# A new table of order, slots and engines for a fused attention and feed-forward kernel

## The chip, the core and the metric

The kernel runs on one core of one Trainium2 chip. The metric is device microseconds of one execution. The core has a matrix engine (TensorE, PE in the profile, with its weight loads as PEld), VectorE (DVE), ScalarE (ACT), GpSimd (POOL) and SyncE (SP, which here only issues DMAs). POOL and ACT issue DMAs too.

## The reference

Random-feature attention over 8 batches and 8 heads of 576 tokens and 64 channels, followed by a feed-forward layer without a gate:

```python
def phi(x):
    proj = np.einsum('bhsd,df->bhsf', x, w_phi)
    proj = proj - np.max(np.abs(proj), axis=-1, keepdims=True)
    return np.concatenate([np.exp(proj), np.exp(-proj)], axis=-1)
q_p, k_p = phi(q), phi(k)
kv = np.einsum('bhsf,bhsd->bhfd', k_p, v)
z = np.sum(k_p, axis=2)
num = np.einsum('bhsf,bhfd->bhsd', q_p, kv)
den = np.einsum('bhsf,bhf->bhs', q_p, z)[..., None] + 1e-06
attn = num / den
...
h = np.maximum(np.maximum(x @ w1, x @ w2), x @ w3)
return h @ w_out
```

`x` is `attn` with 4608 rows (8 batches of 576 tokens) of 512; `w1`, `w2`, `w3` are 512 by 768, `w_out` is 768 by 512.

## The kernel before, in words

**Units and chunks.** The attention is cut into 16 units (two per batch, four heads each) and the feed-forward part into 9 chunks (one per batch of 512 tokens, and a last one of the 64 tokens that are left in each batch). The body of the kernel does not issue instructions: it makes a graph of 1479 steps (`Node`), each with a function that issues its instructions, the engines that may do it, and the buffers that it uses.

**A unit.** q, k and v are loaded (L452 through POOL's queue with a cast to bf16 for units 1 to 3, L463 through SP's queue in f32 for the others and for every v; L441 for the first unit). For units 0 to 3 TensorE turns q and k (L483) and DVE copies them out (L486); for later units POOL casts them (L469) and a DMA turns them (L498). TensorE then projects (L525 and L520, step G), ACT makes exp of k's projections (`Ek`, L538), DVE takes the row maxima of both (L544). From k's maxima ACT makes the factor `em` (L575); v is multiplied by it (`va`, L579, two of 128 by 1152 elements a unit, four of half the width in units 0 and 1), and the factor itself is copied into the 65th column (`vd`, L589). TensorE sums k's features with that product (step K, L633, 72 small matmuls); the result is copied out (`kv`, L638). q's maxima are turned and written into a row of `qkT` by a small DMA (step V, L560), q is projected a second time (L604; L606 and L609 in units 0 and 1) and exponentiated by ACT (`Eq`, L617); TensorE multiplies with `kv` (step N, L651), DVE divides (L657, L658), and the result is turned (L671, or a DMA at L681).

**A chunk.** The maximum of three products is written as w1's product plus the larger of 0, w2's minus w1's, and w3's minus w1's. So `w2 - w1` and `w3 - w1` are formed once (`wd`, L775: three column pieces each, both operands in SBUF), w1 is turned (step wt, L787, copied out by `we`, L790) and multiplied with `w_out` (step wm, L801). A chunk is then 12 steps of four 128x512 matmuls (L704), whose results are cut at 0 (`t1`, L714 on DVE or L712 on ACT) or joined (`h`, L710), and four times a straight product (L732) and a product with `w_out` (L737), copied out (`osb`, L745) and stored (L752).

**The weights** come by four DMAs of 768 KB through POOL's queue with a cast (`w_load`, L413): nodes 1081 (w1), 1082 (w2), 1083 (w3) and 1084 (w_out).

**The order.** A constant string, `PLAN`, holds one word per step. `1087G@37.9` says: node 1087, on POOL (G; T is TensorE, D DVE, A ACT, S SP), at place 37.9; digits and letters between engine and place are the slots of the buffers that it is the first to use. `plan` (L243) reads the words, `fill` (L261) sorts the steps by their places, adds idle 128x512 matmuls (L832) in places where TensorE's row has a hole, and calls the steps' functions in that order. So the numbers after `@` are not waited for: they set each engine's order of instructions, and every engine works through its own order, waiting for what an instruction needs. A DMA's place sets its place in its queue, and SP, POOL and ACT issue in order, too.

**Gates.** v's load of units 1 to 3 is held back by a one-element DVE copy (`gate`, L461, nodes 86, 159 and 231) that writes into v's buffer after an earlier unit's `qkT` is there. SP waits for it before it issues that load and everything behind it.

Of the kernel before, what the change touches and what calls it, by code (L numbers as in the profile page):

```python
# [48 lines left out]
VA_DVE = 1  # L49
# [46 lines left out]
0G@0.5 1G@1.2 4A@2.0 2D0@0.8 10S0@0.7 3D@1.1 11D0@4.2 6S0@1.3 7D@5.0 15T1@5.6 5D@5.5 16D0@6.4 86D0@7.2 26T002300@7.2 12S@1.9  # L96
13A@5.8 8S@2.6 9A@6.5 27A@7.6 28A@8.2 29D@7.6 19T4@7.5 20D@8.2 17T5@7.6 18D@8.4 21T67@8.3 24D@9.0 23A@8.7 41T1@8.6 43A@9.2
22A@9.6 36T24@9.2 37A@10.0 39D@9.6 31T56@9.8 44D@10.3 34D@10.6 32A@10.5 38A@11.0 33A@11.5 25D@11.2 45D@11.8 84G1@1.7
40D@12.1 57T20@11.3 58A@12.0 42A@12.5 85G@2.5 90T5@11.8 91D1@12.8 59A@12.8 14S1@3.2 54T7@12.4 55A@13.3 63T4@12.9 64A@13.8
56A@14.3 35D@13.4 50A0@14.8 65A@15.0 104T111211@13.5 66T5@13.8 158G2@3.4 68A@15.5 108D@14.0 30D@14.6 46A@15.8 88T6@14.1  # L100
89D@15.2 92T7@14.9 93D@15.8 107D@16.0 60T3@15.3 61A@16.1 94T46@16.0 98D@16.6 105A@16.6 67A@17.1 99T71@16.8 102D@17.2
96A@17.4 62A@17.9 97D@17.9 101A@18.4 157G@4.2 163T5@17.6 164D2@18.5 1081G@5.1 1091T7@18.1 1092D0@19.1 109T34@18.7 112D@20.2
161T0@19.0 1084G@5.9 106A@18.9 110A@19.4 95A@19.9 1095T5@19.6 1096A@20.3 114T2@20.0 117D@20.8 116A@21.3 103D@21.2 162D@21.8
111A@21.7 1093T7@20.4 52G0@15.2 47G@16.3 115A@22.1 53G@17.4 49G@17.7 51G@18.0 48G@19.1 69T063@21.0 71A@22.5 133T51@22.1
134A@22.9 70A@23.4 130T0@22.6 159D2@22.4 113D@22.5 118D@23.1 1094D@23.5 100A@23.8 135A@24.3 230G0@20.2 1082G@21.0 229G@21.8
74T30@23.0 75D0@24.6 1083G@22.7 119A1@24.8 122G1@25.1 132A@25.0 78T4@23.4 127T2@23.7 136T6@24.1 137A@25.5 72T1@24.6
73D1@25.2 79D0@25.8 182T007500@25.0 185D@26.5 184A@26.0 138A@26.5 123A@26.9 186D@27.1 1099T3@25.4 1100D@27.7 1101T1@26.7
1102D@28.3 131A@27.2 129A@27.7 177T46@28.1 87S@7.4 120G@25.4 121G@26.5 172T70@28.3 175D@28.9 76T3@28.6 183A@28.2 128A@28.7
165T5@28.9 166D@29.5 178A@29.1 173A@29.6 179A@30.1 139T1@29.1 174A@30.6 1103T2@29.3 140A@31.1 1104A@31.4 180D@29.7 77D1@30.3
181D@31.0 187T7@30.6 191D@31.6 126G@27.7 125G@27.9 124G@29.1 142T154@30.9 176D@31.9 144A@32.1 141A@32.5 143A@32.9 367S1@17.2  # L110
370G1@30.2 167T36@31.9 171D@32.5 195A0@33.3 169A@33.5 189A@34.0 198A0@34.4 188A@34.5 1085G@31.3 235T2@32.3 236D0@33.1
170D@33.7 82T0@32.9 80T4@33.1 81A@34.9 145T11@33.4 146D0@34.3 147T5@33.8 148D1@35.0 190D@35.6 1097T2@34.1 168A@35.5 83A@36.0
1098A@36.6 149T3@35.4 150D0@35.9 151T1@35.7 152D1@36.5 233T4@36.0 234D@37.2 254T115711@36.6 256A@37.1 237T6@37.0 238D@37.8
257D@38.0 153T3@37.1 192T0@37.4 193A0@37.7 231D3@38.6 154A@37.9 155T2@37.5 156A@38.6 255A@39.2 160S@22.6 197G@33.7
244T14@37.9 247D@38.7 196G@35.8 214T006@38.2 216A@39.7 215D@39.4 245A@40.1 249T35@39.2 250A@40.6 252D@39.8 239T21@39.5
242D@40.4 240A@41.1 251A@41.6 258D@41.0 1090D@41.6 241A@42.1 1107T0@39.9 366S1@27.2 259T6@40.8 263D@42.2 1087G@37.9
1115T3@41.0 1116A1@42.5 1108A@43.0 261A@43.5 246A@43.9 1109T2@41.9 253D@42.5 369G@40.0 1088D@43.1 1117T7@42.7 1118A@44.4
302S0@32.6 305G2@41.1 194S@38.1 199T30@43.6 211T5@43.8 212A@44.9 213A@45.4 200A@45.7 243D@43.8 262D@44.4 248D@44.7
1129T0@43.9 1130D@45.3 1086G@42.2 1111T1@44.8 208T7@45.6 1112D@45.9 1110D@46.5 209A@46.2 267A1@46.7 264T4@45.9 265A1@46.9
# [12 lines left out]
412A@65.9 1141A2@66.4 409A@67.0 311D@66.0 330D@66.6 295T5@65.7 411A@67.5 408A@68.0 331D@67.1 296D1@67.4 291T6@66.0
292D0@68.0 1143T4@66.3 289T7@67.2 290D1@68.6 436S0@62.3 303S2@65.2 496S1@65.8 329A@68.5 498S3@66.5 1144T@67.5 1145D3@69.3
308A@68.8 416T1@68.8 418A@69.3 413T5@68.9 415A@69.7 299T2@69.1 300A@70.2 297T6@69.4 298D@69.9 417A@70.8 317T07@69.8
320D@70.4 321D@71.0 695G2@64.4 403G@65.5 401G@65.8 419T034@70.0 421D@71.6 499G0@71.6 332T6@71.2 333D1@72.0 334S@72.3
335A1@71.7 338G1@72.7 337G@73.0 420D@72.2 1155T2@71.2 1167T0@72.1 1156D0@72.6 1168D@73.3 319A@72.0 414A@72.5 318A@73.0
447T001400@73.1 449A@73.5 452T63@73.3 455D@73.9 453A@74.0 437T52@73.5 439A@74.5 448A@75.0 438A@75.5 454A@75.9 440D@74.5
450D@75.1 441D@76.1 1157T7@73.9 1158A@76.4 1165T0@74.7 457T6@75.6 459A@76.9 428T50@75.8 429D0@76.7 566S1@73.0 628S1@75.9
451D@77.3 461D@77.9 1153T1@76.1 1154A@77.3 1166D@78.3 1149T2@77.0 442T75@77.9 443A@78.4 445D@78.9 1150A@78.9 458A@79.4
444A@79.7 336G@75.1 354T114@78.2 356A@80.2 355D@79.5 424T0@79.3 348T21@79.6 349A@80.6 460D@79.9 425D1@80.2 350A@81.2  # L140
627S1@76.5 630G1@82.3 497S0@77.2 500G@83.8 345T7@79.8 456D@80.8 446D@81.4 1169T1@80.1 1170D@82.0 342T6@80.9 587T11411@81.1
343A@81.7 589A@82.2 426T0@81.4 590D@82.7 339T3@81.7 341A@82.5 433S2@77.8 465A0@83.0 467G0@85.3 466G@87.4 340A@83.3 344A@83.8
1146S@79.1 691S0@80.3 694G@89.5 1147T2@81.9 1148D@83.0 422T5@82.7 423D0@83.6 427D1@84.3 430S@85.0 347A@84.2 1159T1@83.1
# [142 lines left out]
def kernel(  # L286
# [133 lines left out]
    def attention(u):  # L420
# [84 lines left out]
        em = buf("em", 2, [P, 2, UT], FP32)  # L505
# [62 lines left out]
        for t0, t1, need in ranges:  # L568
            def va(*args):
                n_va.append(nd(*args))  # L570
                return n_va[-1]
# [10 lines left out]
            for g in range(2):  # L582
                costs = {"POOL": 0.14 + 0.1085 * (t1 - t0)}
                if VA_DVE > u:
                    costs["DVE"] = 0.11 + 0.105 * (t1 - t0)
# [172 lines left out]
    w_nodes = []  # L758
# [105 lines left out]
```

## Time and profile before

| | |
|---|---|
| time, three runs | 291.24, 291.28, 291.81 us; median 291.28 |
| span of the profiled execution, first to last instruction | 290.5 us |
| what lies around the span, against the median | 0.78 us |
| TensorE busy | 276.3 us of the span |
| DVE, ACT, POOL busy | 213.8, 193.8, 116.9 us |

The profile is one execution. Busy time of an engine leaves out the time in which it waits. A window is a stretch of the span; its row gives the busy time of each engine in it with the number of instructions, the granted TensorE clock (1.00 is full speed), the mean busy share of the DMA engines and GB/s. The waits list says who waited for whom: time in total, times, longest. In a timeline row stand start, length, engine, line, operation and tiles; in brackets the idle time ahead of it and what ended it.

### The profile page before, as it was taken

How to read it: one execution, taken by the hardware profiler on the slowest of the kernel's cores; microseconds unless marked ns; L12 is line 12 of the kernel's file. 1: busy time of each engine (PE TensorE's matmuls, PEld its weight loads, DVE VectorE, ACT ScalarE, POOL GpSimd, SP SyncE). 2: the span in 40 equal slices, each digit the busy share in tenths (PEclk: the TensorE clock that was granted, in tenths of full speed). 3: DMA queues.
4: the chain of work that ended last, by engine and by line, in shares of the span. 5: the costliest groups of instructions: out<-in, count | busy, mean ns of one | idle time of the engine just before them, and what ended most of it. 6: DMA issues, size and time to landing. Idle time of an engine off the chain costs nothing.

```text
span 290.5 us, 8509 instructions
## 1 busy us (share of the span) xinstructions
PE 276.3 (95%) x3518; PEld 157.4 (54%) x3555; DVE 213.8 (74%) x449; ACT 193.8 (67%) x446; POOL 116.9 (40%) x99
## 2 busy tenths in 40 slices
PE   8678999899999999999999999999999999999995
PEld 3447676356656655555555566555544654444443
DVE  5695899998998967988979879878963382455411
ACT  1795989789898989976797898858758510021021
POOL 8055789728373662817180753500077001000000
PEclk9997999999999999999999999999999999999999
DMA  7999967899999999997999545982240109414045
GB/s 184 280 242 199 246 198 181 197 360 212 231 241 361 150 257 253 275 262 157 225 324 273 118 83 156 164 167 45 52 115 2 39 10 208 91 39 95 12 122 170
DMA packets 65649, 50.83 MB, mean 175 GB/s; under 512 B 46154, under 2 KB 50378, under 8 KB 65610
## 3 DMA queue, kind: packets, MB, share of 16 engines
q1 hardware_dynamic: 61279, 45.03, 63.2%
q0 software_dynamic: 4000, 4.92, 9.9%
q8 instruction: 28, 0.46, 0.6%
q10 hardware_dynamic: 331, 0.33, 0.3%
q14 instruction: 11, 0.09, 0.1%
HBM read 34.67 MB, written 9.44 MB: 152 GB/s over the span
## 4 chain that ended last, share of the span: by engine, by line
PE 66%; DMA 13%; DVE 10%; POOL 5%; issue 2%; SPq 2%; ACT 2%; ACTq 0%; POOLq 0%; DVEq 0%
PE ups L704 22%; PE ops L737 13%; PE ops L732 9%; DMA w_bf<-in_moe_w_dram 6%; PE psn L651 5%; DMA qkT<-qk_bf 5%; PE kvps L633 5%; PE psm L604 3%; PE psq L525 3%; DVE mk L544 3%; DVE hT L710 2%; POOL vab L579 2%; DMA q_raw<-in_q_dram 2%; DVE mqp L544 2%; PE pm L801 2%
## 5 line engine op out<-in xcount | busy, mean ns | idle before, releaser
L704 PE MATMUL ups<-xT,w_bf 128*128 128x512 bf16 x412 | 101.7, 379 | 2.5 <-DVE mk L544 0.9
L617 ACT ACTIVATE Eq<-psm 128x512 bf16<-128x512 f32 (+1 forms) x160 | 82.3, 584 | 9.6 <-PE psm L604 8.2
L579 POOL TENSOR_TENSOR vab<-v_raw,em 128x1152 bf16<-128x1152 f32 (+1 forms) x36 | 67.9, 1904 | 44.6 <-ACT em L575 31.7
L538 ACT ACTIVATE Ek<-psk 128x512 bf16<-128x512 f32 x128 | 70.6, 616 | 8.3 <-PE psk L525 5.1
L704 PEld LDWEIGHTS <-w_bf 128*128 128x128 bf16 x432 | 40.6, 98 | 47.2 <-issue 2.3
L544 DVE TENSOR_REDUCE mqp<-psq 128x4 bf16<-128x512 f32 (+1 forms) x80 | 48.8, 632 | 8.3 <-PE psk L525 4.9
L737 PE MATMUL ops<-wout_bf,hT 128*128 128x512 bf16 (+1 forms) x215 | 50.4, 373 | 0.4
L710 DVE TENSOR_TENSOR hT<-hT,ups 128x512 bf16<-128x512 bf16 x54 | 35.9, 681 | 12.3 <-PE ups L704 8.5
L544 DVE TENSOR_REDUCE mk<-psk 128x4 f32<-128x512 f32 x64 | 42.6, 682 | 1.8 <-PE psk L525 1.1
L745 ACT COPY osb<-ops 128x512 f32<-128x512 f32 (+1 forms) x18 | 10.5, 590 | 38.2 <-PE ops L737 35.7
L737 PEld LDWEIGHTS <-hT 128*128 128x128 bf16 x222 | 21.0, 98 | 22.3
L658 DVE TENSOR_TENSOR x_sb<-psn,rden 128x320 bf16<-128x320 f32 x64 | 31.5, 491 | 2.2
L712 ACT ACTIVATE hT<-ups 128x512 bf16<-128x512 f32 x32 | 19.8, 627 | 17.2 <-PE ups L704 17.2
L651 PEld LDWEIGHTS <-Eq 128*128 128x128 bf16 x640 | 25.2, 97 | 7.7
L651 PE MATMUL psn<-kv_sb,Eq 128*128 128x65 bf16 x640 | 27.3, 194 | 0.0
L745 DVE COPY osb<-ops 128x512 f32<-128x512 f32 (+1 forms) x19 | 12.8, 673 | 19.5 <-PE ops L737 16.4
L732 PE MATMUL ops<-xT 128*128 128x512 bf16 x89 | 24.0, 380 | 0.4
L525 PE MATMUL psq<-w,qkT 64*128 64x128 bf16 x256 | 21.5, 219 | 0.8 <-DMA qkT<-qk_bf 0.8
L604 PE MATMUL psm<-qkT,wphi_m 128*128 128x512 bf16 (+1 forms) x70 | 22.3, 358 | 0.0
L525 PE MATMUL psk<-w,qkT 64*128 64x128 bf16 x256 | 21.4, 219 | 0.0
L714 DVE TENSOR_SCALAR hT<-ups 128x512 bf16<-128x512 f32 x22 | 14.8, 685 | 8.4 <-PE ups L704 8.4
L633 PE MATMUL kvps<-vab,Ek 64*128 64x65 bf16 x1152 | 20.1, 190 | 0.4 <-POOL vab L579 0.4
(76 smaller groups left out, 266.7 us busy)
## 6 DMA issues: line engine op xcount, KB each, us to landing
v_raw<-in_v_dram SPq DMA_DIRECT2D x16, 576.0 KB, 5.4
out_dram<-osb SPq DMA_DIRECT2D x66, 128.0 KB, 2.4
k_raw<-in_k_dram SPq DMA_DIRECT2D x12, 576.0 KB, 4.5
q_raw<-in_q_dram SPq DMA_DIRECT2D x12, 576.0 KB, 6.0
w_bf<-in_moe_w_dram POOLq DMA_DIRECT2D x3, 768.0 KB, 17.0
qk_bf<-in_q_dram POOLq DMA_DIRECT2D x3, 288.0 KB, 10.9
qk_bf<-in_k_dram POOLq DMA_DIRECT2D x3, 288.0 KB, 10.7
wout_bf<-in_moe_w_out_dram POOLq DMA_DIRECT2D x1, 768.0 KB, 21.0
```

The costliest lines, as they stand in the source:

```text
L525: nc.tensor.matmul(ps()[:, i, :], lhsT=cols[r, :], rhs=w2[r, c, :], start=True, stop=True)
L538: nc.scalar.activation(Ek[s]()[:, tiles_of(t0, n), :], of(1), EXP, scale=1.0 - 2.0 * s)
L544: nc.vector.tensor_reduce((mq, mk)[c]()[:, tiles_of(t0, n)], of(c), AXX, ALU.max, apply_absolute_value=True)
L579: (nc.vector if n_.eng == "DVE" else nc.gpsimd).tensor_tensor(vab()[:, g, t0:t1, 0:D], vb()[:, t0:t1, :], em()[:, g, t0:t1].unsqueeze(2).t ...
L617: nc.scalar.activation(Eqb()[s][:, cols], psm()[:, 0:w], EXP, scale=1.0 - 2.0 * s)
L633: nc.tensor.matmul(kvps[ab]()[:, t // NT, g, :], lhsT=Ek[g]()[r, t, :], rhs=vab()[r, g, t, :], start=(t + g == 0), stop=(t == UT - 1 and g ...
L651: nc.tensor.matmul(psn()[:, c, :], lhsT=Eqb()[g][:, t0:t0 + P], rhs=kv()[:, pr, ab, g, :], start=(g == 0), stop=(g == 1))
L658: nc.vector.tensor_tensor(x_sb()[:, pr, :, ab, :], psn()[:, :, 0:D], rden().to_broadcast([P, 5, D]), ALU.mult)
L704: nc.tensor.matmul(ups(), lhsT=w_bf[i + 1][:, ct, j * P:(j + 1) * P], rhs=tokens_of(ct), start=(ct == 0), stop=(ct == CT - 1))
L710: nc.vector.tensor_tensor(hT()[:, j, :], hT()[:, j, :], ups(), ALU.max)
L732: nc.tensor.matmul(ops_()[:, 0:width], lhsT=tile_of(ct, tt), rhs=line_w[c_i > MOVE][:, ct, cols], start=(ct == 0), stop=False)
L737: nc.tensor.matmul(ops_()[:, 0:width], lhsT=hT()[:, j, tt * P:(tt + 1) * P], rhs=wout_bf[:, j, cols], start=False, stop=(j == JT - 1))
```

## The change

All words of `PLAN` are replaced; two kinds of steps get more engines to choose from. Nothing else in the code differs, and the arithmetic is the same. The table is cut here to the words that the texts speak of:

```diff
-VA_DVE = 1
...
 PLAN = """
-... 84G1@1.7 ... 85G@2.5 ... 158G2@3.4 ... 157G@4.2 ... 1081G@5.1 ... 1084G@5.9 ... 230G0@20.2 ... 1082G@21.0 ... 229G@21.8 ... 1083G@22.7 ...
-... 86D0@7.2 ... 87S@7.4 ... 367S1@17.2 ... 159D2@22.4 ... 160S@22.6 ...
+... 84G0@1.9 ... 85G@2.6 ... 1081G@3.3 ... 157G1@4.0 ... 158G@4.7 ... 1084G@5.5 ... 1082G@6.2 ... 229G2@11.4 ... 230G@12.1 ... 1083G@12.8 ...
+... 86D1@20.2 ... 87S@20.4 ... 159D2@20.9 ... 367S1@20.9 ... 160S@21.3 ... 432S0@21.8 ... 366S1@22.2 ...
...
             for g in range(2):
-                costs = {"POOL": 0.14 + 0.1085 * (t1 - t0)}
-                if VA_DVE > u:
-                    costs["DVE"] = 0.11 + 0.105 * (t1 - t0)
+                costs = {"POOL": 0.14 + 0.1085 * (t1 - t0), "DVE": 0.11 + 0.064 * (t1 - t0)}
                 n_ = va("va", costs, None, [n_em, mains[2]], [vb, em, vab])
...
-            n_ = va("vd", {"ACT": 0.15, "POOL": 0.28}, None, [n_em], [em, vab])
+            n_ = va("vd", {"ACT": 0.15, "POOL": 0.28, "DVE": 0.15}, None, [n_em], [em, vab])
...
-            n_ = node("wd", 0, {"DVE": 0.6} if i else {"POOL": 2.1}, None, [w_nodes[0], w_nodes[i + 1]], [])
+            n_ = node("wd", 0, {"DVE": 1.2, "POOL": 2.1}, None, [w_nodes[0], w_nodes[i + 1]], [])
```

What the two tables say, counted:

| step | before | after |
|---|---|---|
| `va`, product of v (L579) | POOL 36 | POOL 29, DVE 7 (one each in units 8, 9, 10, 11, 14, two in unit 15) |
| `vd`, copied column (L589) | POOL 9, ACT 9 | POOL 9, ACT 6, DVE 3 |
| `wd`, weight differences (L775) | POOL 3, DVE 3 | POOL 5, DVE 1 |
| `kv` (L638) | DVE 17, ACT 15 | DVE 7, ACT 25 |
| `t1` (L714, L712) | DVE 22, ACT 32 | DVE 18, ACT 36 |
| `osb` (L745) | DVE 19, ACT 18 | DVE 16, ACT 21 |
| casts of unit 0 (L445) | DVE 2, ACT 2 | ACT 4 |
| step V's DMA (L560) | SP 13, ACT 1 | SP 10, ACT 4 |
| last chunk's stores (L752), and idle matmuls (L832) | 1 on ACT; 23 | 3 on ACT; 31 |

Order in the queues at the start, read from the two built programs:

| queue | before | after |
|---|---|---|
| POOL's DMAs | two loads of unit 1, two of unit 2, w1, w_out; then, behind unit 0's four `va`: unit 3's k, w2, unit 3's q, w3 | two loads of unit 1, w1, two of unit 2, w_out, w2, two of unit 3, w3; then unit 0's `va` |
| SP, behind unit 0's loads | v of unit 1 (gate 86, seventh of DVE's steps), k of unit 5, v of unit 2 (gate 159), q of unit 5, k of unit 4 | v of unit 1 (gate 86, 26th of DVE's steps, behind most of unit 1's maxima), k of unit 5, v of unit 2, k of unit 6, q of unit 5 |

288 lines of the change are left out of this document (147 added, 141 removed).

## Prediction

> **What bounds the kernel now.** I read the page first, then the windows, to see in which part of the span TensorE is not full. The page has a span of 290.5 us, against a median time of 291.28 us; the 0.78 us between them is taken as what lies around the span, and put back at the end.
>
> ```profile
> span 290.5 us, 8509 instructions
> PE 276.3 (95%) x3518; PEld 157.4 (54%) x3555; DVE 213.8 (74%) x449; ACT 193.8 (67%) x446; POOL 116.9 (40%) x99
> PEclk9997999999999999999999999999999999999999
> ```
>
> ```profile
> core 0: us, PE busy (x) PEld busy (x) DVE busy (x) ACT busy (x) POOL busy (x), PEclk, DMA share, GB/s
> 8.00:20.40 12.40, 9.81 (x167) 6.21 (x167) 10.10 (x20) 11.16 (x28) 2.68 (x5) 1.00 1.14 266
> 20.40:27.00 6.60, 4.16 (x55) 3.34 (x50) 2.80 (x5) 3.11 (x7) 5.03 (x6) 0.74 1.20 199
> 27.00:70.00 43.00, 41.44 (x739) 26.30 (x743) 40.46 (x85) 38.73 (x95) 29.77 (x22) 1.00 0.91 230
> 70.00:150.00 80.00, 78.36 (x1149) 46.39 (x1157) 69.66 (x154) 69.11 (x162) 43.04 (x33) 1.00 1.00 251
> 150.00:245.00 95.00, 93.83 (x1183) 52.72 (x1196) 69.65 (x146) 63.57 (x147) 30.54 (x23) 1.00 0.53 110
> ```
>
> From 27 us on TensorE is idle for 1.56 of 43, 1.64 of 80 and 1.17 of 95 us: it is the bound, and its work is the same in both tables, so no order can win more than some 4 us there. The weak place is the window from 20.4 to 27: 4.16 busy of 6.60, at a mean clock of 0.74, with DVE and ACT mostly idle as well. The timeline and the waits of that stretch say why.
>
> ```profile
> 22.98 0.77 PEld L787 LDWEIGHTS <-w_bf 128*128 128x128 bf16 x8 [2.60 <-DMA w_bf<-in_moe_w_dram]
> ...
> 27.01 1.27 PE L633 MATMUL kvps<-vab,Ek 64*128 64x65 bf16 x72
> ```
>
> ```profile
> 4.96 17.97 DMA w_bf<-in_moe_w_dram
> ```
>
> ```profile
> ACT Ek L538 <- PE psk L525: 2.7, 1, 2.7
> DVE hT L790 <- PE pwT L787: 2.5, 1, 2.5
> DVE mqp L544 <- PE psq L520: 1.3, 1, 1.3
> ACT hT L790 <- PE pwT L787: 0.7, 1, 0.7
> ```
>
> TensorE stands for 2.60 us in front of the first turning of w1 (L787); w1 was issued at 4.96 and landed 17.97 us later, at 22.93. ACT and DVE run dry behind it. Unit 0's K (L633), the mark by which I compare the two tables, starts at 27.01.
>
> **The change, part by part.**
>
> *A, the start.* The new table issues w1 third on POOL's queue instead of fifth, and holds v of unit 1, and so all loads behind it on SP, until the 26th of DVE's steps, instead of the seventh. What the queues moved, in the DMA view cut to 0 to 10.5, 10.5 to 18.5, 18.5 to 23 and 30 to 42 us (packets, MB, share; q0 is POOL's queue, q1 SP's):
>
> ```profile
> q1 hardware_dynamic: 793, 1.67, 52.6%
> q0 software_dynamic: 439, 0.49, 29.4%
> ...
> q0 software_dynamic: 796, 0.92, 66.2%
> q1 hardware_dynamic: 597, 1.28, 46.7%
> ...
> q0 software_dynamic: 748, 0.93, 118.3%
> ...
> q0 software_dynamic: 903, 1.22, 56.9%
> q1 hardware_dynamic: 816, 1.77, 41.8%
> ```
>
> A load of a unit's q or k is 0.295 MB in q0, a weight 0.786. Before, w1 ends at 4 x 0.295 + 0.786 = 1.97 MB: 0.49 + 0.92 are done at 18.5, the rest at 0.93 / 4.5 = 0.207 MB/us takes until 21.2, and the landing is seen 1.7 us later. After, w1 ends at 2 x 0.295 + 0.786 = 1.38 MB. The 1.28 MB of q1 from 10.5 to 18.5 are mostly the two loads that are now held, so q0 has the DMA engines to itself: 10.5 + 0.89 / 0.207 = 14.8, landing at about 16.5. With q1 as busy as before it would be 10.5 + 0.89 / 0.115 + 1.7 = 19.9. The turning stands three steps earlier in TensorE's order, which was done with all in front of it at 20.38, so it comes to it little before 17, and the 2.60 us go.
>
> The lost clock goes with it: (1 - 0.74) x 6.60 = 1.7 us. Together 4.3. What is late next are ACT and DVE: the table asks for as many DVE steps ahead of unit 0's K as before (31), and ACT was 11.16 of 12.40 busy ahead of the stall. They can only win what they waited: ACT 2.7 + 0.7, DVE 2.5 + 1.3. I take **-3.7**, near the 3.8 of DVE; bounds -4.3 and -1.3 (w1 at 19.9, a stall and a slow clock remain). [...]
>
> *B, differences off DVE.* Two of three `wd` leave DVE.
>
> ```profile
> 47.96 0.96 DVE L775 TENSOR_TENSOR w_bf<-w_bf 128x1024 bf16<-128x1024 bf16 x1
> 49.77 1.68 DVE L775 TENSOR_TENSOR w_bf<-w_bf 128x1024 bf16<-128x1024 bf16 x1
> 55.29 1.63 DVE L775 TENSOR_TENSOR w_bf<-w_bf 128x1024 bf16<-128x1024 bf16 x1
> ...
> 47.23 1.15 POOL L469 CAST qk_bf<-k_raw 128x1152 bf16<-128x1152 f32 x1
> 48.34 2.57 POOL L775 TENSOR_TENSOR w_bf<-w_bf 128x1024 bf16<-128x1024 bf16 x1
> 50.85 1.60 POOL L469 CAST qk_bf<-k_raw 128x1152 bf16<-128x1152 f32 x1
> 54.26 2.12 POOL L579 TENSOR_TENSOR vab<-v_raw,em 128x1152 bf16<-128x1152 f32 x1 [1.80 <-ACT em L575]
> ```
>
> ```profile
> 52.20 1.02 PE L704 MATMUL ups<-xT,w_bf 128*128 128x512 bf16 x4 [0.88 <-DVE mk L544]
> ...
> PEld L704 <- issue: 1.9, 3, 1.3
> ```
>
> Each difference on DVE ends 0.54 us after POOL's instruction that was running (48.38, 50.91, 56.38): it waited 0.42, 1.14 and 1.09 us. Behind the second stood a `mk` maximum, and TensorE stood 0.88 to 1.3 us at 52.2. I take **-1.2** (bounds -1.3; 0 if another wait ends there). The three pieces on POOL in a row cost it 2.12 each; it is idle for 13 of 43 us there.
>
> *C, the loads that were held.* Five loads of 0.59 MB now start together at about 20.5, while q0 still has 4.92 - 0.49 - 2.07 = 2.36 MB to move. At the 1.22 / 12 = 0.102 MB/us that q0 got beside a busy q1, w_out (it ends at 2.75 MB, 0.19 after the 2.56 that are through at 20.5) lands at 20.5 + 1.9 + 1.7 = 24.1; its first user, L801, stands one projection behind K, 23.3 + 1.27. q1's 2.95 MB at 1.77 / 12 = 0.148 take until 40.4, when q0 still has 0.33 MB; w3, its last, lands at 40.4 + 1.6 + 1.7 = 43.7. The first difference of w3 stood at 47.96 and comes 3.7 earlier, at 44.3. That is just enough: **+0.5**, bounds 0 and +2.5.
>
> *D, products on DVE.*
>
> ```profile
> L579 POOL TENSOR_TENSOR vab<-v_raw,em 128x1152 bf16<-128x1152 f32 x28 | 58.9, 2121 | 33.5 <-ACT em L575 20.5 <-issue 10.6 <-DMA v_raw<-in_v_dram 2.4
> L658 DVE TENSOR_TENSOR x_sb<-psn,rden 128x320 bf16<-128x320 f32 x64 | 31.5, 491 | 2.2
> L710 DVE TENSOR_TENSOR hT<-hT,ups 128x512 bf16<-128x512 bf16 x54 | 35.9, 681 | 12.3 <-PE ups L704 8.5 <-ACT hT L712 2.9 <-ACT Eq L617 0.6
> L638 DVE CAST kv_sb<-kvps 128x260 bf16<-128x260 f32 x17 | 7.1, 421 | 4.6 <-PE kvps L633 4.5
> L714 DVE TENSOR_SCALAR hT<-ups 128x512 bf16<-128x512 f32 x22 | 14.8, 685 | 8.4 <-PE ups L704 8.4
> ```
>
> 320 elements take 491 ns and 512 take 681: 0.99 ns an element, so 1152 would take about 1.31 us (0.6 at the rate of the bf16 difference; 1.31 + 2.12 behind a whole product on POOL). Seven of them are 9.2 us of DVE, against some 12 moved off it (net ten `kv` of 0.42, four `t1` of 0.69 and three `osb`, taken alike, and two `wd` of 0.96 to 1.68). Behind each wait stand maxima and divisions. It matters where K follows closely: in unit 9 both products start on the same `em`, one on each engine, so one waits for the other. **+0.5**, bounds 0 and +2.6. [...]
>
> *E, ACT.* From 27 to 110 us it has the steps that the table takes off DVE.
>
> ```profile
> 27.00:110.00 83.00, 80.65 (x1332) 50.19 (x1344) 75.78 (x164) 74.44 (x178) 54.11 (x39) 1.00 0.95 238
> ...
> L638 ACT CAST kv_sb<-kvps 128x260 bf16<-128x260 f32 x15 | 5.8, 388 | 3.9 <-PE kvps L633 3.9
> ...
> 214.05 1.34 ACTq L560 DMA_DIRECT2D qkT<-mT  x1
> ```
>
> Counted up to the third chunk's first product, it gets three more `kv` (1.2 us), three exponentials and two copies (an estimate of 2.7, at 0.39 to 0.69 each), and issues two V DMAs (2 x 1.34): 6.6 us into the 8.6 that it had idle. Every later step of its queue waits behind them. **+0.5**; bounds +4, and -1 since DVE, which was 91% busy, is relieved.
>
> The last stores on ACT and eight more idle matmuls lie in waits: 0. Sum: -3.7 - 1.2 + 0.5 + 0.5 + 0.5 = **-3.4**: a span of 287.1, and 291.28 - 3.4 = 287.9.
>
> **The rivals.** (1) *More comes off*: ACT and DVE carry the start to the full 4.3 and C to E cost nothing: -5.6, 285.7; with half of TensorE's other idle time after 27 us (some 1.5), 284.2. For it: TensorE's row has no other long wait. Against it: E's thin margin. (2) *The weights come earlier, but the held loads give most of it back*, since the same bytes have to be in by 42 us: C at +2.5, 289.9. For it: the DMA share is 0.91 to 1.20 up to 150 us. (3) *The change does not do what it says*: gate or queue order has no effect on w1's landing, A is 0, and B pays D and E: 291.28 - 1.2 + 1.5 = 291.6. Against it: both queues issue in order. (4) *ACT becomes the bound* between 27 and 110, and it is slower. ACT keeps all of its 8.6 us of waits, having room for 2.0: the stretch is 6.6 longer, 291.28 - 3.9 + 6.6 = 294.0. It decides from 5.9 us of waits left there: 2.0 fit, 3.9 cancel A to D. For it: ACT works in order, and its waits were for TensorE. Against it: those waits shrink when TensorE is earlier. [...]
>
> **How the numbers follow.** Forecast 0.50 (286.5 to 289.2), (1) 0.14, (2) 0.14, (3) 0.05, (4) 0.10, (5) 0.07. The predicted time is 287.9. The range, 284.4 to 291.4, takes in the forecast, (2), most of (1) and part of (3), about 0.8. Faster by over 0.2% (0.6 us, about what a measurement of this kernel can tell from no change): 0.50 + 0.14 + 0.14 = 0.78; the same 0.05; slower 0.17.
>
> **What would show it.** A: the wait for w1 at L787 is gone or under 0.5 us, the clock is 1.00 from 8 us on, unit 0's K starts near 23.3 instead of 27.0. B: no wait over 1 us at L704 near 48. C: waits of L801 for w_out and of L483 for unit 3's loads under 0.5 us each. D: products on DVE at 1.3 us alone, up to 3.4 beside POOL's. E: ACT's waits from 23 to 106 us at 2 to 3 us. The prediction is wrong if K of unit 0 is early and the lead of 3.7 us is gone by the third chunk: then it was ACT or the held loads, and the waits say which.

## The result, and the profile after

The changed kernel takes 295.03 us (median of four runs, 294.41 to 295.74) beside 291.36 of the kernel before (291.24 to 291.81): a ratio of 1.0113 (1.0078 to 1.0148). That is 3.3 us slower by the ratio, 3.7 by the two medians; the text goes on with the ratio. The forecast was 287.9, with a range up to 291.4. Single executions of one kernel differ by 1% and more (290.3 to 294.3 us for the kernel before on one chip), so the verdicts below go by the ratios to the kernel before on the same chip, each with its 95% interval, and the traces only tell where time goes.

The page and the windows of the changed kernel, against those of before:

```profile
span 294.0 us, 8533 instructions
PE 276.8 (94%) x3525; PEld 157.3 (54%) x3563; DVE 213.6 (73%) x434; ACT 200.9 (68%) x466; POOL 108.3 (37%) x94
PEclk9999999999999999999999999999999999999999
```

```profile
core 0: us, PE busy (x) PEld busy (x) DVE busy (x) ACT busy (x) POOL busy (x), PEclk, DMA share, GB/s
8.00:20.40 12.40, 11.66 (x192) 7.35 (x192) 11.23 (x24) 11.11 (x29) 7.07 (x9) 1.00 1.18 225
20.40:27.00 6.60, 5.03 (x143) 3.92 (x139) 5.38 (x11) 6.24 (x14) 0.00 (x0) 1.00 1.15 244
27.00:70.00 43.00, 37.64 (x638) 23.75 (x644) 35.34 (x77) 34.25 (x83) 33.69 (x24) 1.00 0.99 271
70.00:150.00 80.00, 76.61 (x1106) 44.85 (x1112) 69.22 (x136) 69.49 (x165) 38.19 (x29) 1.00 0.91 224
150.00:245.00 95.00, 93.72 (x1218) 53.44 (x1230) 74.56 (x151) 67.89 (x158) 21.65 (x17) 1.00 0.58 118
```

The start went as forecast: the clock stays at full speed (1.00 in every window), and w1 is turned from 17 us on, with 0.17 us of wait. Unit 0's K starts at 22.81 instead of 27.01. But TensorE is idle for 5.36 of the 43 us from 27 on (1.56 before) and for 3.39 of the next 80 (1.64). DVE and ACT are busy for less of the window from 27 to 70 than before (35.34 and 34.25 beside 40.46 and 38.73), so neither of them is full there. Lines of the changed kernel are those of before plus 3 or 5. Rows of the changed kernel's timeline, what TensorE waited for in it from 20 to 150 us, and the row of before that answers to the first of these waits:

```profile
17.25 0.61 PE L790 MATMUL pwT<-ident,w_bf 128*128 128x128 bf16 x8
17.26 0.43 PEld L790 LDWEIGHTS <-w_bf 128*128 128x128 bf16 x7 [0.17 <-issue]
...
22.81 1.27 PE L636 MATMUL kvps<-vab,Ek 64*128 64x65 bf16 x72
```

```profile
PEld L530 <- issue: 6.0, 14, 1.6
PEld L607 <- DMA qkT<-mT: 3.6, 2, 2.8
...
PEld L636 <- issue: 2.5, 3, 1.7
PEld L488 <- issue: 2.1, 3, 1.2
...
PEld L636 <- DVE x_sb L661: 1.0, 2, 0.9
PEld L525 <- DMA qkT<-qk_bf: 1.0, 1, 1.0
```

```profile
PEld L525 <- issue: 5.3, 13, 0.4
```

Before, the unnamed waits of step G were never longer than 0.4 us, and TensorE waited for no V. The chain of work that ended last, followed back from the last instruction, has three pieces of TensorE called "issue" of over 1 us, which means that TensorE waited for nothing that the profile names (a fourth, at 100.31, is POOL's and is shown under what stays open), and step V's small DMAs (`qkT<-mT`):

```profile
24.19 1.52 issue
...
39.79 1.01 issue
...
44.62 1.55 issue
...
55.16 6.11 DMA qkT<-mT
```

To compare stages, I paired the steps of the table with the instructions of the trace, in order. Start of a step in us (K of a unit; a chunk's first product with w2's difference), in one profiled execution each; the kernels named e5 to e17 come below:

| | K u0 | K u2 | K u3 | chunk 3 | chunk 4 | K u12 | K u15 |
|---|---|---|---|---|---|---|---|
| before | 27.0 | 44.4 | 65.6 | 109.6 | 143.0 | 196.0 | 228.3 |
| after | 22.8 | 43.4 | 64.7 | 110.8 | 145.4 | 200.4 | 231.7 |
| e5, start alone | 22.7 | 41.7 | 63.1 | 106.3 | 140.8 | 194.4 | 226.5 |
| e12, products alone | 25.5 | 43.4 | 64.4 | 108.7 | 144.7 | 199.2 | 231.1 |
| e10, quiet V | 22.4 | 42.3 | 61.4 | 107.5 | 142.5 | 201.4 | 232.7 |
| e17, edges moved | 22.9 | 41.7 | 61.2 | 109.1 | 144.5 | 199.5 | 230.7 |

Two executions differ by 1 us and more even where the code is the same: e12 has the start of before, and its first K is 1.5 us earlier. A lead of 4.2 us at unit 0's K is 1.0 at unit 2's, gone by the third chunk, and a loss of 4.4 at unit 12's.

### The profile page after: what moved, and what is told of

It is laid out like the page before. It is cut to its first block, busy times and chain, and to the rows that moved or that the text cites. A ratio compares the mean times of both kernels' runs of the same rounds, so it can differ in the third digit from the quotient of the medians.

```text
span 294.0 us, 8533 instructions
## 1 busy us (share of the span) xinstructions
PE 276.8 (94%) x3525; PEld 157.3 (54%) x3563; DVE 213.6 (73%) x434; ACT 200.9 (68%) x466; POOL 108.3 (37%) x94
## 4 chain that ended last, share of the span: by engine, by line
PE 72%; DMA 10%; DVE 7%; issue 5%; POOL 3%; ACT 1%; SPq 0%; ACTq 0%
PE ups L707 27%; PE ops L740 12%; PE ops L735 8%; DMA qkT<-mT 5%; PE psn L654 5%; PE kvps L636 5%; PE psm L607 4%; PE psq L530 3%; PE idler L835 3%; DMA qkT<-qk_bf 3%; POOL vab L584 2%; DVE mk L549 2%; DMA q_raw<-in_q_dram 2%; POOL qk_bf L474 1%; DVE mqp L549 1%
## 5 line engine op out<-in xcount | busy, mean ns | idle before, releaser
L620 ACT ACTIVATE Eq<-psm 128x512 bf16<-128x512 f32 (+1 forms) x160 | 80.7, 584 | 7.1 <-PE psm L607 7.1
L543 ACT ACTIVATE Ek<-psk 128x512 bf16<-128x512 f32 x128 | 73.5, 622 | 11.9 <-PE psk L530 5.9
L584 POOL TENSOR_TENSOR vab<-v_raw,em 128x1152 bf16<-128x1152 f32 (+1 forms) x29 | 53.4, 1853 | 64.5 <-ACT em L580 29.0
L740 PE MATMUL ops<-wout_bf,hT 128*128 128x512 bf16 (+1 forms) x217 | 51.3, 373 | 0.3 <-issue 0.2
L748 ACT COPY osb<-ops 128x512 f32<-128x512 f32 (+1 forms) x21 | 12.2, 593 | 32.6 <-PE ops L740 21.4
L715 ACT ACTIVATE hT<-ups 128x512 bf16<-128x512 f32 x36 | 21.7, 620 | 18.1 <-PE ups L707 17.6
L717 DVE TENSOR_SCALAR hT<-ups 128x512 bf16<-128x512 f32 x18 | 12.1, 684 | 15.4 <-PE ups L707 15.4
L636 PE MATMUL kvps<-vab,Ek 64*128 64x65 bf16 x1152 | 20.7, 190 | 2.6 <-issue 1.6
L636 PEld LDWEIGHTS <-Ek 64*128 64x128 bf16 x1152 | 19.0, 94 | 5.1 <-issue 3.3
```

Of the source, the lines that this page charges most:

```text
L543: nc.scalar.activation(Ek[s]()[:, tiles_of(t0, n), :], of(1), EXP, scale=1.0 - 2.0 * s)
L584: (nc.vector if n_.eng == "DVE" else nc.gpsimd).tensor_tensor(vab()[:, g, t0:t1, 0:D], vb()[:, t0:t1, :], em()[:, g, t0:t1].unsqueeze(2).t ...
L620: nc.scalar.activation(Eqb()[s][:, cols], psm()[:, 0:w], EXP, scale=1.0 - 2.0 * s)
L636: nc.tensor.matmul(kvps[ab]()[:, t // NT, g, :], lhsT=Ek[g]()[r, t, :], rhs=vab()[r, g, t, :], start=(t + g == 0), stop=(t == UT - 1 and g ...
L740: nc.tensor.matmul(ops_()[:, 0:width], lhsT=hT()[:, j, tt * P:(tt + 1) * P], rhs=wout_bf[:, j, cols], start=False, stop=(j == JT - 1))
```

## The experiments

Two theories for what took the lead, beside the rivals of the prediction. Theory 1: the three unnamed waits are blocks of instructions that come late; an edge is the place where one block ends and the next begins. Theory 2: V's small DMA has too little room in the new order. The rivals: DVE's steps held up beside POOL's products (the prediction's fifth, 294.4 us), ACT as the bound, the held loads. In the diffs a word is that of the table; only words that change are shown.

**e1, the unnamed waits by themselves.** A kernel of small matmuls alone.

```diff
+for n_sp, n_pool in ((0, 0), (8, 0), (0, 8), (6, 6)):   # loads beside the stretch
+    for i in range(1152): nc.tensor.matmul(ps[i % 2][:, c], lhsT=ek[r, :], rhs=va[r, :])
```

> This kernel leaves the whole computation out and writes constants: it has four stretches of 1152 small matmuls each (64 by 128 weights, 65 columns, as in step K, each with its own weight load), the first with no loads beside it, the second beside eight f32 loads of 0.59 MB on SP's queue, the third beside eight cast loads on POOL's queue, the fourth beside six of each. Theory 1 (TensorE's instructions come in blocks of 256 by a queue of their own, the fetch of the next block starts only when a block is entered, and loads in flight delay it): in the changed kernel three blocks were usable 1.4 to 1.6 us after their 16 KB had arrived, and arrived 3.9 to 4.4 us after the block before was entered, so a block of 256 lasts at least 5.3 us beside loads. A step K of 144 instructions took 1.15 us, so 256 need 2.05 us when nothing is late: I expect a wait of about 3 us at each block in the second to fourth stretches (45 us or more for 2304 instructions), and shorter ones or none in the first (18.4 us without any wait; about 27 us if an undisturbed fetch takes 3 us). Rival (the three waits of the changed kernel were for data that the profile does not name): every stretch runs at 18 to 20 us with no wait at a block's edge.

The timeline of the first stretch (two rows), the second (three) and the third (one), and the windows inside these stretches:

```profile
23.07 2.12 PE L105 MATMUL ps<-va,ek 64*128 64x65 bf16 x128 [1.61 <-issue]
26.80 2.12 PE L105 MATMUL ps<-va,ek 64*128 64x65 bf16 x128 [1.61 <-issue]
...
41.17 2.15 PE L105 MATMUL ps<-va,ek 64*128 64x65 bf16 x128 [0.66 <-issue]
47.09 2.86 PE L105 MATMUL ps<-va,ek 64*128 64x65 bf16 x128 [3.77 <-issue]
53.01 1.23 PE L105 MATMUL ps<-va,ek 64*128 64x65 bf16 x38 [3.07 <-issue]
...
85.03 3.18 PE L105 MATMUL ps<-va,ek 64*128 64x65 bf16 x128 [4.35 <-issue]
```

```profile
8.00:38.00 30.00, 18.56 (x1132) 1.00 0.02 4
40.30:53.00 12.70, 5.22 (x270) 0.81 0.97 368
...
78.00:91.30 13.30, 5.37 (x260) 0.79 1.11 178
```

In the first stretch a wait stands after every 128 weight loads and 128 matmuls: 1.61 us in the two rows, 11.4 us in eight waits, with no loads beside it (3.73 from edge to edge in these rows; the stretch took 30 us, not 18). Beside loads the waits in the rows are 0.66 us as the loads begin, then 3.07 to 4.35: from edge to edge 5.92 with SP's loads and, with the 2.12 of work, some 6.5 with POOL's. The block and the delay by loads are shown; the expectation of 27 us or less for the first stretch was too low.

**e2, a wide step into the wait at 24 us; e3, unit 3's V earlier; e8, three mends at once.**

```diff
 # e2
-182T007000@24.2 ... 1099T3@24.5
+1099T3@24.15 182T007000@24.2
 # e3
-264T7@49.1 265D1@49.9 266A@50.2
+264T6@47.0 265D1@47.05 266A@47.25
 # e8: as e2 and e3, and a wide step ahead of unit 2's K
-214T075@40.3 1107T7@42.3
+1107T5@40.25 214T71@41.15
```

> The changed kernel with one step of six wide matmuls (wm, node 1099) moved ahead of the G step of unit 2 (node 182) that it stood behind; nothing else. Theory 1 (the wait of 1.52 us inside that G step, at 24.2, was for a block of instructions, which arrives at a fixed time after the block before was entered): the wide step fills the wait, the wait at 24.2 falls from 1.5 to under 0.3 us, and the second projection of unit 2 is done 1.2 to 1.5 us earlier; as DVE and ACT may take part of that up, the whole is 0.5 to 1.4 us faster than the changed kernel, 293.6 to 294.5 on the median of 295.0. Rival (the wait was for data of unit 2 or for a slow neighbour): the G step waits as before behind the wide step, and the time stays at 295.0 or grows.

> The changed kernel with unit 3's maxima turned, copied out and written by its small DMA 2.1 to 3 places earlier in the table (264, 265, 266 from 49.1, 49.9 and 50.2 to 47.0, 47.05 and 47.25); the DMA stays on ACT's queue. Theory 2 (the wait of 2.8 us at 61.3 is a DMA that needs 6.1 us beside a busy queue where the table leaves 3.6): the DMA is issued near 52.5 instead of 55.16 and lands by 59, the wait falls to under 0.7 us and the kernel gains 1.5 to 2.7 us: 292.3 to 293.5. Rival A (DVE or ACT are the bound there, as the prediction's fourth rival had it): TensorE waits as long for something else, Eq or h, within 5 us, and the time stays within 0.5 of 295.0. Rival B (the DMA only lands when the queue of SP's loads is empty, whenever it is issued): it is issued earlier and lands at 61 still, and nothing is gained.

> The changed kernel with three mends in one: the wide wm step 1099 ahead of the G step of unit 2; a wide up step (1107) ahead of unit 2's K, with that step's banks changed accordingly; unit 3's maxima turned, copied and sent 2 to 3 places earlier, the words put in order of place so that no idle matmul is added (in the run that moved unit 3's alone, two idle matmuls came in at 48 and 49, one of them stood 1.3 us for its bank, and most of the gain went there). Theories 1 and 2: the waits of 1.5 at 24.2 and 1.6 at 44.6 fall to under 0.5 each, that of 2.8 at 61.3 to under 0.7, together 4.5 us; if later waits stay as they are, 290.5 to 292.5 on the median of 295.0, ratio to before 0.997 to 1.004. Rival (another engine or the loads bound that stretch, so that each mend is given back at the next wait): the third chunk starts no more than 1.5 us earlier than in the changed kernel, and the ratio stays over 1.006.

e2 1.0110 (1.0025 to 1.0195), e3 1.0103 (1.0064 to 1.0141), e8 1.0109 (1.0056 to 1.0161): nothing gained. In e2 the wait at 24 us fell from 1.52 to 0.47 (under 0.3 was expected) and K of unit 2 came 1.8 us earlier, and none of it was left at the end. In e8 the wide step ran into the same edge (0.93 us of "issue" inside it at 25.97), so moving a step within a block hides little. In e3 the wait for unit 3's DMA went, but two idle matmuls had come in, and one of them stood 1.27 us for its bank (`<-ACT Ek L543`). In e8 the waits at 44 and 61 went, and waits for ACT (`Eq`, 1.2; `kv`, 0.7) and for the DMAs of units 7, 10 and 13 (3.5) took their place.

**e4, e5, e6, e9: the start alone, on the old order.**

```diff
 # e4: w1 third, loads held
-86D0@7.2 87S@7.4 158G2@3.4 157G@4.2 1081G@5.1 367S1@17.2 159D2@22.4 160S@22.6 366S1@27.2
+1081G@3.0 158G2@3.4 157G@4.2 86D0@17.55 87S@17.75 367S1@18.3 159D2@18.55 160S@19.0 366S1@19.9
 # e5: POOL's whole queue as in the change; 86, 87, 367, 159, 160 as in e4
-158G2@3.4 157G@4.2 1081G@5.1 1084G@5.9 230G0@20.2 1082G@21.0 229G@21.8 1083G@22.7
+1081G@3.0 158G2@4.0 157G@4.7 1084G@5.5 1082G@6.2 230G0@12.1 229G@12.8 1083G@13.4
 # e6: as e5, but 86, 87, 159, 160, 367 as before
 # e9: as e5, but w2 behind unit 3
-1082G@6.2
+1082G@13.0
```

> The kernel before with only the start of the change: w1 third on POOL's queue, and gate 86 and the SP loads behind it held until the 26th of DVE's steps (part A and most of part C alone: four loads start together at about 20). Prediction's own sum for A and C: -3.7 + 0.5, a median of 288.1 beside 291.36; unit 0's K near 23.3. Theory 1 (bulk loads that start together delay the blocks of instructions): K of unit 0 is early, but where small matmuls are dense between 20 and 46 us waits of 1 us and more without a named cause appear; 288.5 to 290.5. Rival (all of the loss in the changed kernel is in its order behind the start, none in the held loads): 287.4 to 288.2, with no wait over 0.5 us between 23 and 48 us other than those of before.

> The kernel before with the whole start of the change and nothing behind it: POOL's queue in the new order (unit 1, w1, unit 2, w_out, w2, unit 3, w3, all ahead of unit 0's products), gates 86 and 159 and the loads behind them at the new places. In the run that moved w1 alone and held the loads, unit 0's K came 3.4 us earlier and then TensorE stood 4.2 us for unit 3's q, which was still queued behind the products on POOL. Theory (the start itself is sound once unit 3's loads are issued early, and the changed kernel lost its time by the order behind the start): no wait over 1 us at unit 3's turning near 35, unit 0's K 3 to 3.7 us earlier than before, a median 2 to 3.5 us under that of before. Rival 1 (the bytes that have to be in by 42 us set the time, whatever the order): the wait moves to v of units 1 or 2, k of unit 5 or w3, and the time is within 0.7 us of before. Rival 2 (blocks of instructions that come late beside the loads): waits of 1 us and more without a named cause between 20 and 48 us, 1 to 3 us of the lead lost by 50 us.

> The same with the gates and SP's loads left where they stood before: only POOL's queue is changed. Theory: w1 lands later than with the held loads (near 19.9 by the prediction's bound, since SP's queue has half of the DMA engines), unit 0's K 1.3 to 3 us earlier than before, but v of units 1 and 2 and k of unit 5 are in early, so less has to be moved between 20 and 42 us: 1.3 to 3 us under before. Rival (held loads are needed for w1): w1 lands at 21 or later, the wait for it stays over 1 us, and no more than 1 us is gained.

> The kernel before with the start of the change, as in the run that gave 0.9952 of before, but with unit 3's two loads ahead of w2 in POOL's queue. There TensorE still stood 1.1 us at 35.9 for unit 3's q. Theory (the lead of the start is kept as far as each load lands in time): that wait goes, w2 lands some 6 us later than in that run but its first difference has room; 0.3 to 1 us more, ratio to before 0.990 to 0.996. Rival (w2 is then what is late): no wait for unit 3's q, but waits of the wide steps for the weight differences near 44 to 48 us of 1 us and more, ratio 0.995 to 1.000.

e4 1.0029 (0.9995 to 1.0062), e5 0.9952 (0.9908 to 0.9997), e6 1.0023 (0.9992 to 1.0054), e9 0.9940 (0.9910 to 0.9970). TensorE's wait for unit 3's q, in e4 and in e5:

```profile
PEld L489 <- DMA qk_bf<-in_q_dram: 4.3, 1, 4.3
```

```profile
PEld L483 <- DMA qk_bf<-in_q_dram: 1.1, 1, 1.1
```

w1 alone with held loads only moves the wait to the next load. With unit 3's loads early too, the start is worth 0.5 to 0.6%, and holding SP's loads is part of it: without that (e6) no gain shows. The prediction's second rival, that the held loads give the lead back, is the wrong way round.

**e7 and e12: the products of v, taken off DVE in the new order, put on DVE in the old one.**

```diff
 # e7, on the changed kernel (e12: the same ten on D, on the kernel before, at its own places)
-126D 533D 596D 598D 662D 727D 791D 987D 1051D0 1052D
+126G 533G 596G 598G 662G 727G 791G 987G 1051G0 1052G
```

> The changed kernel with the seven products and three copied columns of DVE given back to POOL at the same places; the rest of the new table stays. [...] Theory 1 says nothing here: the block waits at 24, 39 and 44 us stay as they are.

> The kernel before with only the new engines of the products: the same seven products and three copied columns on DVE, at the places of the old table; order, start and loads stay. [...] Rival (the loss in the changed kernel by these products came only from its tighter order): no difference, 0.998 to 1.002.

e7 1.0067 (1.0030 to 1.0104), less than half a per cent under the change, with intervals that overlap; the wait of 0.9 us at unit 9's K went. e12 1.0109 (1.0070 to 1.0149): the products and columns alone, with the order of before, cost 3.2 us, as much as the whole change. In e12's row of the table the distance to before hardly moves up to the third chunk (from -1.5 to -0.9); the next two columns lose 2.6 and 1.5. Pieces of its chain that ended last, where they go through DVE, and TensorE's waits for a division (`x_sb`), of which before has none of over 0.2 us:

```profile
102.73 1.35 DVE vab L579
104.21 0.49 DVE x_sb L658
...
133.06 2.67 DVE vab L579
136.80 0.49 DVE x_sb L658
...
151.55 1.42 DVE vab L579
...
175.44 1.47 DVE vab L579
177.05 0.50 DVE x_sb L658
```

```profile
PEld L651 <- DVE x_sb L658: 1.1, 1, 1.1
PEld L633 <- DVE x_sb L658: 0.9, 2, 0.5
...
PEld L525 <- DVE x_sb L658: 0.6, 1, 0.6
```

Four products, 6.9 us, stand on the chain, three of them ahead of divisions, and TensorE waits 2.6 us for divisions. Only one of the four (2.67) met a whole product on POOL; a copied column did, too, and lasted 1.40 us instead of 0.24, of which 0.85 stand on the chain. In the changed kernel TensorE's wait for divisions is 1.0 us (`L636 <- DVE x_sb`), so the price on the old order is not the price in the change.

**e10, e13, e14, e16: step V's small DMA.** Theory 2 (room): the new table leaves less between V and its user. By place, V to first user: 3.6 to 11.3 (middle 5.5) before, 2.6 to 7.1 (middle 4.2) after; the DMA lands 4.4 to 6.1 us after its issue at units 3, 7 and 13.

```diff
 # e10, on the changed kernel: bulk transfers behind unit 3's V (266A@50.2)
-563S0@46.7 496S1@47.2 498S2@48.1 431S0@48.8 306S2@49.9 497S1@52.7
+306S2@54.0 563S0@54.3 496S1@54.6 498S2@54.9 431S0@55.2 497S1@55.5
 # e13, on the changed kernel (e14: the reverse, on the kernel before; e16: e13 and e7)
-306S2@49.9 266A@50.2 334A@76.8 529A@113.8 919A@149.7
+266S@50.2 306S2@50.25 334S@76.8 529S@113.8 919S@149.7
```

> The changed kernel with six transfers of SP's queue (v of unit 8, k, q and v of unit 7, q of unit 6, and the turning of unit 4's k and q) moved from places 46.7 to 52.7 to 54.0 to 55.5, behind the small DMA of unit 3 (place 50.2, on ACT's queue), which itself stays. Theory 2 (a small DMA lands in 2.3 us in a quiet queue, as unit 14's did at 217, and in 4.5 to 6.1 beside bulk transfers; the table leaves it 3.6): issued near 55.2 as before, it lands by 59, and the wait of 2.8 us at 61.3 falls under 1 us. Rival A (the DMA is slow of itself on ACT's queue): it still lands 6 us after its issue and the wait stays over 2 us. On the whole time: units 6 to 8 get their data up to 3 us later, so 0 to 2 us better than the changed kernel, ratio to before 1.004 to 1.012.

> The changed kernel with the V steps of units 3, 4, 7 and 13 back on SP's queue (unit 4's turning one step behind unit 3's V). Queue theory (a DMA from ACT's queue lands later beside SP's bulk transfers): the waits for units 3, 7 and 13 fall from 2.8, 0.8 and 0.3 to under 0.5 each, landing 4.0 to 4.6 us after the issue; 1 to 3 us better than the changed kernel, ratio 1.001 to 1.008. Room theory (the new table leaves 3.4 to 4.6 between V's place and its user, the old one 3.6 to 11.3, and any queue needs 4 to 6 us there): the waits stay within 0.7 us of what they were, ratio 1.008 to 1.014.

> The kernel before with the V steps of units 3, 4, 7 and 13 on ACT's queue, at the same places. Queue theory: units 7 and 13, which have 4.5 and 4.1 us there between issue and user, wait 0.5 to 2 us more, ratio 1.002 to 1.010. Room theory: same landing as from SP's queue, waits under 0.5, ratio 0.998 to 1.002.

> The changed kernel with both: the four V steps on SP's queue and the products and copied columns of DVE back on POOL (alone 1.0067). If both theories hold and add: 0.996 to 1.003. If the rest sits in the order of TensorE's steps (blocks of instructions at 24, 39 and 44 us, room of the small DMAs): 1.004 to 1.010.

e10 1.0119 (1.0065 to 1.0173), e13 1.0591 (1.0521 to 1.0661), e14 0.9995 (0.9961 to 1.0028), e16 1.0559 (1.0496 to 1.0622). In e10 the wait for unit 3's V fell from 2.8 to 1.6 us (under 1 was expected). TensorE's waits for V, in e13 from 20 to 245 us and in e10 from 150 to 175:

```profile
PEld L607 <- DMA qkT<-mT: 17.6, 5, 6.8
```

```profile
PEld L607 <- DMA qkT<-mT: 4.8, 2, 3.3
```

On the old order ACT's queue shows no cost (e14). SP's queue is far worse in the new order: unit 3's V was issued there at 53.74, behind six loads issued in the 3.5 us ahead of it, and took 8.90 us. That these loads are the reason is read from the order of the queue. In e10 the third chunk is 3.3 us ahead of the changed kernel, and the waits for V of units 10 and 13 (1.6 and 3.3 us; unit 13's took 7.4 us from issue to user) take it all back. With SP's queue that much worse, e16 cannot tell whether gains add up; beside e13 it is a second reading of the products on the new order, 0.3% better, with intervals that overlap.

**e11, products and mends together; e17, the edges of the blocks moved.**

```diff
 # e11: e7's words, and those of e8 without e2's
 # e17: cut the first 22 idle matmuls of the start, 132 instructions more
+for c in range(4):
+    nc.tensor.matmul(idler[:, c * P:(c + 1) * P], lhsT=idle, rhs=idle, start=True, stop=True)
```

> The changed kernel with the products and copied columns of DVE given back to POOL (alone: 1.0067 of before), unit 2's K behind a wide step and unit 3's maxima sent earlier (with the moved wm step, these two alone: 1.0109). [...] Rival (each mend is given back at the next wait: ACT and DVE near 50 us, the small DMAs of units 7, 10 and 13): 1.004 to 1.010, with waits for those DMAs of over 3 us in all.

> The changed kernel with the first 22 idle matmuls of the start (128 by 512) cut into four of 128 by 128 each, and nothing else: the same idle work while TensorE waits for its first data, but 132 more instructions ahead of all others, so that every edge between blocks of 256 comes 132 instructions earlier in the work. Worked out from the changed kernel's trace (its own steps without the three waits, and 5.4 us at least from edge to edge): the three waits at 24, 39 and 44 us, 4.3 us, go down to 0.1 in all. Theory 1: no wait over 0.3 us without a named cause between 20 and 50 us, the third chunk 2 to 4 us earlier, and of that 0 to 3 us kept at the end (the small DMAs took most of earlier mends): ratio to before 1.001 to 1.011. Rival (the waits belong to the steps: data, banks or clock): waits of 1 to 1.6 us in the same G, T and K steps as before, ratio as it was, 1.008 to 1.015.

e11 1.0128 (1.0078 to 1.0177), e17 1.0127 (1.0086 to 1.0168). e11 lies above the 1.004 to 1.010 expected of it, and above e7 (1.0067), whose words it has; beside e8 (1.0109, with e2's word besides) it is a third reading of the products on the new order, and shows no gain. In e17, the window from 20.4 to 27, the longest wait without a name from 20 to 50 us, and the waits from 50 to 150:

```profile
20.40:27.00 6.60, 6.55 (x180) 5.18 (x176) 6.57 (x15) 6.54 (x17) 0.00 (x0) 1.00 1.15 246
```

```profile
PEld L488 <- issue: 0.9, 2, 0.5
```

```profile
PEld L607 <- DMA qkT<-mT: 2.9, 4, 1.1
PEld L530 <- DMA qkT<-qk_bf: 2.8, 2, 2.4
...
PEld L525 <- DMA qkT<-qk_bf: 1.9, 1, 1.9
```

The three waits were edges: with the edges elsewhere the same G, T and K steps run through. And they were not the price: e17 is 3.5 us ahead at unit 3's K, 1.7 at the third chunk, 0.9 at the fourth, keeps 1.0 at unit 15's K in this trace, and nothing by the ratio. What takes the lead back are the DMAs that turn units 5 and 9 (2.4 and 1.9) and four V's.

**e15 and e18: the best version.** e9, with one weight difference off DVE; then its edges moved as in e17.

```diff
 # e15, on e9; e18: e15 with e17's code
-1088D@43.1
+1088G@45.0
```

> The version with the start alone and unit 3's loads first (0.994 of before), with one weight difference (node 1088) moved from DVE to POOL, behind POOL's cast at 45. There one difference lasted 2.56 us on DVE for the two beside POOL's 2.12, and TensorE stood 1.15 us at 49.1 for a maximum behind them. Term B of the prediction (two of three off DVE: -1.2): this one gives -0.3 to -1, ratio 0.990 to 0.994. Rival (POOL's casts and products of units 3, 4 and 6 come 2.1 us later and something waits for them): 0.994 to 1.000.

> The best version so far (the start of the change on the old order, unit 3's loads ahead of w2, one weight difference on POOL; 0.9906 of before) with its 23 idle matmuls of the start cut in four in the same way (138 more instructions). Its trace had no wait over 0.5 us at an edge, but it crossed two of them (25.9, 39.5) just when the block became usable, 1.5 us after it had arrived. Theory: 0 to 1 us better, ratio 0.987 to 0.992. Rival: the start is later by the cut matmuls, or the edges fall on denser steps: 0.992 to 0.998.

e15 0.9906 (0.9867 to 0.9945), e18 0.9903 (0.9868 to 0.9938). Both beat both kernels, by 2.7 us against before and some 6 against the change. One difference off DVE is worth about 1.0 us by the two ratios (0.9940 and 0.9906), but their intervals overlap, so the gain is not shown. Moving the edges is worth nothing here, where TensorE waited at none of them for over 1 us.

## Why the prediction was wrong, step by step

**Where the difference lies.** The forecast was -3.4 us, and the ratio gives +3.3. Of the 6.7 us between them, 1.8 lie in A and C (forecast -3.2 together, -1.4 in e5). D was entered at +0.5; it measures 3.2 on the old order (e12) and 1.3 on the new one (e7, not clear of the noise), so it holds 0.8 to 2.7. The other 2.2 to 4.1 lie in the rest of the new table: the sum had -0.7 for it (B and E) and put the new order of the steps at nothing without a reason, and by the runs that rest costs 1.5 to 3.4. These are differences of ratios that are each known to some 0.4%.

**A, the start** (-3.7). The mechanism was right in each point: no wait for w1, full clock (1.00), K at 22.81 (forecast 23.3). The size was not, and this step of the prediction failed: a lead at unit 0's K was entered in the sum as if it reached the end. Made alone, start and held loads together give -1.4 (e5, 0.9952 of 291.4; -2.7 to -0.1), not -3.2.

**B, differences** (-1.2). The wait at L704 near 48 is gone, as forecast. For one difference e15 gives about -1.0, not clear of the noise; for two nothing was measured.

**C, held loads** (+0.5). No wait for w_out or unit 3's q in the changed kernel. Holding them pays (e5 against e6).

**D, products on DVE** (+0.5, bounds 0 and +2.6): the second step that failed, as far as the old order shows it. e12 measures +3.2 (2.0 to 4.3). On the new order e7, e16 and e11 give 0.5%, 0.3% and -0.2%, none clear of the noise. The duration was right (forecast 1.31; 1.35 measured), and in the changed kernel one product and one copied column (0.24 us alone) were held up beside a whole product of POOL:

```profile
116.16 1.75 DVE L592 CAST vab<-em 128x36 bf16<-128x36 f32 x1
...
136.09 2.12 POOL L584 TENSOR_TENSOR vab<-v_raw,em 128x1152 bf16<-128x1152 f32 x1 [1.00 <-ACT em L580]
136.24 3.18 DVE L584 TENSOR_TENSOR vab<-v_raw,em 128x1152 bf16<-128x1152 f32 x1
```

What was wrong is the netting: 9.2 us onto DVE against 12 off it, so little. e12 took nothing off DVE, but its chain shows the price: a product stands as a block of 1.35 to 2.7 us ahead of divisions, and is paid where TensorE waits for those next. That the 12 us came off at places where they do not make up for it is a reading, not shown.

**E, ACT** (+0.5). Not the bound: 10.8 us idle from 27 to 110 where 2.0 were forecast, and TensorE waited for ACT 0.6 us in all from 20 to 150. No run gave ACT's added steps back to DVE, so what they cost by way of other engines is not measured.

```profile
27.00:110.00 83.00, 77.11 (x1208) 47.30 (x1221) 69.00 (x149) 72.16 (x173) 54.51 (x38) 1.00 0.95 248
```

**Rivals.** (4) gave 294.0, near the result; as far as the runs show, that is luck: TensorE hardly waited for ACT, and the rival's test, ACT's idle time, cannot tell ACT as the bound from ACT waiting for a late TensorE. (5), 7 us for eight of DVE's steps that wait 2.12 us each beside POOL's products, gave 294.4 and is near it by luck, too. It had the engine that e12 shows, but no run shows such a wait at each of them: in the changed kernel the products on DVE last 1.36 us in the middle and one 3.18, in e12 1.42 and one 2.76. The price in e12 was DVE's order more than these waits, and e7 does not give the 7 us back. (1) fell with e5, (3) with the wait for w1, which went as A said, (2) with e6.

**What no term held.** The prediction read the old trace for engines, and the new table only where it touched them. Nothing in it priced how much room the new order leaves to latencies: blocks of instructions and V's DMA, whose places it could have compared. Its closing test was half right: the lead was gone by the third chunk, but it was not the held loads (e5, e6), and TensorE hardly waited for ACT.

**What stays open.** Start and products together make 0.9952 x 1.0109 = 1.0060, if the two multiply; the change has 1.0113. The rest of the new order costs between 0.5% by that and 1.15% by e7 (1.0067 against 0.9952): 1.5 to 3.4 us. Which step of the new order costs it is not known: every single wait that was mended there was given back at a later one (e2, e3, e8, e10, e11, e17). One long piece of the changed kernel's chain goes through POOL and a turning DMA:

```profile
100.31 5.48 issue
105.79 2.12 POOL vab L584
107.91 1.93 POOL qk_bf L474 x2
109.83 7.72 DMA qkT<-qk_bf
```

TensorE waits 1.0 us at its end (`L525 <- DMA qkT<-qk_bf`). The chain of before has such a DMA as well (8.30 us at 118.55). That POOL's products and casts ahead of the turning DMAs, and the DMA share of 0.91 to 0.99 up to 150 us, set the later waits is a reading of the chain, not shown.

## What to carry to other kernels

Where a table of an order is replaced, compare the room that each latency gets in the old and the new one (small DMAs, turning DMAs, loads), not only the busy time of the engines. Work moved to an engine is priced by what stands behind it in that engine's order, at its place, and not against what left the engine elsewhere. A lead at an early mark is not yet a gain at the end: here 4.3 us at the first K (e5) left 1.4.

## What the runs showed of the hardware

TensorE gets its instructions in blocks of 256: in e1 a wait stands after every 128 weight loads and 128 matmuls, and its page has 36 instruction packets, 0.59 MB in all, for 4632 weight loads and 4632 matmuls. A stretch of small matmuls runs out of them: 3.73 us from edge to edge with nothing beside it, where the work is 2.12, 5.92 beside bulk loads from SP's queue and some 6.5 beside those from POOL's (e1), so the cost is not hidden there. That it is hidden where 256 instructions last longer than that is an estimate: 128 wide matmuls, at 0.22 us each (1.73 for eight in the changed kernel's chain), last some 28 us.

In e1 the granted clock was 1.00 beside waits of 1.61 us and 0.79 to 0.81 in the windows with waits of 3.1 to 4.4. In the kernel before it was at half (0.50) from 22.8 to 26.2 us, behind the wait of 2.60 us for w1; in the changed kernel it stayed at 1.00 behind the wait of 2.83 us at 61.3.

A DMA of 4.5 KB took at most 2.3 us from issue to its user in a quiet stretch of the changed kernel (unit 14, 216.94 to 219.28 us, at a DMA share of 0.24) and 8.9 behind bulk loads of its own queue (e13).
